# Two decode layers streamed through SBUF: one array for all records, more columns kept, a smaller ring and finer w2 pieces

## The chip, the cores and the metric

The kernel runs on one core of one Trainium2 chip. The time is device microseconds of one execution. Times of several executions are given as their median with the lowest and the highest.

## The reference

Four tokens (batch B = 4, one position each, D = 640) go through attention, an MLP, the same attention and the same MLP again; both rounds use the same weights and the same caches. All is float32.

```python
x = A_x
x = x + A(_layernorm(x));  x = x + B(_layernorm(x))
x = x + A(_layernorm(x));  x = x + B(_layernorm(x))

# A: 32 heads of 128; the last W = 1024 positions of each cache
q = x @ wq                                   # 640 x 4096
scores = einsum("bhqd,bhkd->bhqk", q, k) * 128 ** -0.5
o = einsum("bhqk,bhkd->bhqd", softmax(scores), v)
return o.reshape(B, 1, 4096) @ wo            # 4096 x 640
# B: w1 is 640 x 1728, w2 is 1728 x 640
return maximum(x @ w1, 0) @ w2
```

## The kernel before

**Records.** Everything that one head needs is one *record* of 128 partitions x 9472 columns of float32 (`REC`): 640 columns of query weights (from `WQ` = 0), 4096 of keys (from `K` = 640), 4096 of values (from `V` = 4736) and 640 of output weights (from `WO` = 8832). In HBM the array `rec` has one block per head, [32, 128, 9472], so that two partitions' rows of one record lie 9472 x 4 = 37,888 bytes apart. The MLP's weights are one array `wm` of 128 x 17280 columns: five chunks of w1 with 1728 columns each and then 54 tiles of w2 with 160 columns each (`FD`).

**Places.** SBUF holds five slots of one record each (`slot0` to `slot4`), a `ring` of 5344 columns, `kept` with the last 2176 columns of record 26 and `kept2` with the last 1664 columns of record 5. Round 0 goes through the records 0 to 31. Its last five (27 to 31) stay in the slots and are the first five of round 1, which then goes through 0 to 26; so they are loaded once, and what lies in `kept` and `kept2` isn't loaded a second time either.

**Loads.** All loads are issued by SP's queue in one fixed order, the list `items`. `pump()` (line 250) issues the list's first entry as soon as no live columns lie in its place, and stops at the first that has no room yet. `done()` (line 271) frees columns after the last instruction that reads them and calls `pump()`. Around the first MLP the places are few, because the slots hold the five records that stay: `MLP_RING` (line 69) cuts `wm` into 11 pieces that pass through the ring and through `spare`, 1536 columns of the values of record 31, which `park()` (line 290) copies into PSUM and `unpark()` (line 298) brings back later into the keys' columns of slot 2. `IN_RING` and `IN_SLOT` (lines 74 to 76) then place record 0 of round 1 in ring, spare and slots, and the loop over `places` (lines 225 to 238) fills the slots' parts with records 1 to 5 as they are freed. `ending()` (line 190) orders the last three records of a round in parts, so that their keys come ahead of their values.

**Compute.** Each engine runs its instructions in the order in which the program states them (`InOrder`, line 84). For each record `query` makes q by five matmuls with the record's query weights, `scores` makes eight matmuls with the keys, `softmax` is a maximum on VectorE and an exponential on ScalarE, `weights` transposes and scales the probabilities, `values` makes eight matmuls with the values, `picks` and `output_T` gather the head's output, and `project` adds its product with the output weights to `acc`. The main loop (line 469) runs these one record apart: scores of the next record, then values of this one, then the query of the one after. `busy` (line 315) issues matmuls whose result nobody reads; they read the keys of slot `home(LAST, 0)`, which is slot 2, or another one that is named.

`mlp` (line 417) goes through w1's chunks, then through w2 in groups of tiles: `W2_RING` (line 68) in round 0, `W2_SLOT` in round 1.

Of the kernel before, what the change touches and what calls it, by code (L numbers as in the profile page):

```python
# [32 lines left out]
F32 = mybir.dt.float32  # L33
# [5 lines left out]
P = 128  # L39
B, D, H, DH, W, FF = 4, 640, 32, 128, 1024, 1728  # L40
NB = 4
FD = D // NB
# [4 lines left out]
WQ, K, V, WO = 0, D, D + 4 * W, D + 8 * W  # L47
REC = 2 * D + 8 * W
HALF = REC // 2
VH = 2 * W  # L50

NS = 5
# [5 lines left out]
TCOLS = len(TILES) * FD  # L58
RING = 5344
KEPT = WO - 3 * 512  # L60
SIXTH = 5
KEPT2 = WO - 2 * 512
PARKED = 1536
# [14 lines left out]
CUTS = [*range(0, K, DH), *range(K, WO, 512), *range(WO, REC + 1, FD)]  # L78
W1_SLOT = [[0, 1], [2], [3], [4]]
# [26 lines left out]
def decode_kernel(ctx: ExitStack, tc: tile.TileContext, xf, rec, wm, out):  # L106
# [64 lines left out]
    def home(h, r):  # L171

        return h % NS if not r or h >= LAST else (h - 6 + LAST) % NS

# [3 lines left out]
    live = []  # L178
    spare = home(H - 1, 0)
    buffers = dict(enumerate(slot)) | {"ring": ring, "kept": kept, "kept2": kept2}  # L180

    def load(key, src, lo, hi, buf, col):
        if buf == "spare":
            buf, col = spare, V + col
        items.append((key, src, lo, hi, buf, col))

    def piece(r, h, lo, hi, buf=None, col=None):
        load(("rec", r, h), rec[h], lo, hi, home(h, r) if buf is None else buf, lo if col is None else col)

    def ending(r, hs, late):  # L190
        a, b, c = hs[-3:]
        end = WO if late else REC
        last = WO if late else KEPT
        for h, lo, hi in ((a, 0, V), (b, 0, V), (a, V, end), (c, 0, V), (b, V, end), (c, V, V + VH), (c, V + VH, last)):
            piece(r, h, lo, hi)
        if late:
            for h in hs[-1:] + hs[-LATE:-1]:
                if h == LAST - 1:
                    piece(r, h, WO, REC, "kept", WO - KEPT)
                else:  # L200
                    piece(r, h, WO, REC)
# [12 lines left out]
    for lo, hi, buf, col in MLP_RING:  # L214
        load(("w", 0), wm, lo, hi, buf, col)

# [5 lines left out]

    for lo, hi, buf, col in IN_RING:
        piece(1, new[0], lo, hi, buf, col)
    places = [(old[i], lo, hi) for i, lo, hi in (
        (0, 0, K), (0, K + 1024, K + VH), (0, K + VH + 512, V), (1, 0, K + VH), (1, K + VH, V), (0, V, WO), (0, WO, REC),
        (2, 0, V), (1, V, REC), (3, 0, V), (2, V, REC), (4, 0, V), (3, V, REC), (4, V + PARKED, REC),
        (4, V, V + PARKED))] + [("ring", 0, RING)]
    stream = [(new[0], lo, hi) for lo, hi in IN_SLOT] + [(h, 0, KEPT2 if h == SIXTH else REC) for h in new[1:6]]
    for buf, lo, hi in places:  # L230
        while stream:
            h, c, end = stream[0]
            cut = max(x for x in [*CUTS, end] if x <= min(end, c + hi - lo))
            if cut <= c:
                break
            piece(1, h, c, cut, buf, lo)
            lo += cut - c
            stream[:1] = [(h, cut, end)] if cut < end else []
    assert not stream
# [3 lines left out]
    for ks in W1_SLOT:  # L243
        load(("w", 1), wm, ks[0] * FF, (ks[-1] + 1) * FF, home(LAST + 1, 0), ks[0] * FF)
    n = 0
    for size in W2_SLOT:
        load(("w", 1), wm, W2 + n * FD, W2 + (n + size) * FD, home(LAST + 2, 0), n * FD)
        n += size

    def pump():  # L250

        while items:
            key, src, lo, hi, buf, col = items[0]
            if any(b == buf and x < col + hi - lo and col < y for b, x, y in live):
                return
            sp.dma_start(buffers[buf][:, col:col + hi - lo], src[:, lo:hi])
            live.append((buf, col, col + hi - lo))
            at.setdefault(key, []).append((lo, hi, buf, col))
            items.pop(0)
# [30 lines left out]
    def park(i):  # L290
        if i == 0:
            act.copy(sc_ps[1], slot[spare][:, V:V + 1024])
        else:
            act.copy(o_ps, slot[spare][:, V + 1024:V + PARKED])
            free(spare, V, V + PARKED)
            pump()

    def unpark(i):
        b = home(LAST, 0)
        a = [K, K + 512, K + VH][i]  # L300
        if i == 0:
            act.copy(slot[b][:, a:a + 512], sc_ps[1][:, :512])
        else:
            dve.tensor_copy(slot[b][:, a:a + 512], [sc_ps[1][:, 512:], o_ps][i - 1])
        live.append((b, a, a + 512))
        if i == 2:
            dve.memset(o_ps, 0.0)
            at["rec", 1, H - 1] = [(0, V, spare, 0), (V, V + 1024, b, K), (V + 1024, V + PARKED, b, K + VH),
                                   (V + PARKED, REC, spare, V + PARKED)]

# [3 lines left out]

    def busy(n, to=misc, groups=1, h=LAST):
# [29 lines left out]

    def query(r, h):
# [4 lines left out]
        dve.tensor_copy(qT, misc[:, 8:8 + B])  # L351

    def scores(r, h, s, first=False):
        key = ("rec", r, h)
        for i in range(2):
            for b in range(B):
                pe.matmul(sc_ps[s][32 * b:32 * b + 4, 512 * i:512 * i + 512], qT[:, b:b + 1].to_broadcast([P, 4]),
                          cols(key, K + 512 * (B * i + b), 512), start=True, stop=True)
# [58 lines left out]
    def mlp(r):  # L417
# [38 lines left out]
    for r in range(2):  # L456
# [4 lines left out]
        if r:  # L461
            busy(256, t_ps, 2)
        scores(r, hs[0], 0, True)
# [5 lines left out]
        for n, h in enumerate(hs[:-2]):  # L469
# [3 lines left out]
            softmax(s)  # L473
            end = n == H - 3
            values(r, h)
            if end:
                for _ in range(3):
                    busy(512)
            picks(0)
            query(r, hs[n + 2])  # L480
            if end:
                scores(r, hs[-1], 1)
                weights(s, (0,))
            if r and n < NS - 2:
                busy(256, sc_ps[n % 2], 2, H - 1)
            output_T(max(i, 0), by_act=end)
# [65 lines left out]
```

## Time and profile before

| | |
|---|---|
| median of 3 runs | 714.66 us (713.81 to 715.4) |
| profiled execution, its own time | 713.95 us |
| its span, first to last instruction | 712.2 us |
| busy: PE, PE weight loads, VectorE, ScalarE | 512.9, 208.7, 358.5, 95.9 us |
| DMA | 302.53 MB, mean 425 GB/s |
| mean granted TensorE clock | 0.805 |

Busy times are unions over the whole span and overlap one another. All instructions bear line 98 (or 95), where the helper `InOrder` issues them, so groups are told apart by the names of the tiles that they write and read (out<-in). `slot<-rec` is a load of a record's columns into a slot, `ring<-wm` one of MLP weights into the ring. `PEclk` is the granted clock as a share of full speed.

### The profile page before, as it was taken

The numbers are of one execution on the slowest core, as the hardware profiler recorded it, in microseconds if no ns is written. First come the engines' busy times: TensorE is split into PE (matmuls) and PEld (weight loads), VectorE is DVE, ScalarE is ACT, GpSimd is POOL, SyncE is SP. The second block draws the span as 40 slices with busy tenths as digits, with TensorE's granted clock in tenths as the row PEclk, the third lists the DMA queues.
The fourth block names the chain that finished last, engine by engine and source line by source line (L and its number), as shares of the span: only waits on it lengthen the run. The fifth ranks groups of instructions, "written<-read, shape, count | busy, mean of one in ns | idle before, by whom it ended". The sixth has DMA issues, their size and how long they took to land.

```text
span 712.2 us, 8977 instructions
## 1 busy us (share of the span) xinstructions
PE 512.9 (72%) x3718; PEld 208.7 (29%) x3718; DVE 358.5 (50%) x1008; ACT 95.9 (13%) x152; POOL 1.1 (0%) x9
## 2 busy tenths in 40 slices
PE   4466668676586756768989899776858666677976
PEld 2132223223233222323223333232323222233322
DVE  3335444544454545447541877744445544444761
ACT  1201010110101011011120321201010110101111
POOL 0000000000000000000000000000000000000000
PEclk9778786877876687678899999976686878866899
DMA  9999999999999999999999999999999999999996
GB/s 375 443 435 426 428 437 440 418 437 438 433 420 443 433 429 428 430 436 428 424 403 396 418 432 428 441 432 433 433 434 433 430 431 435 432 431 425 429 424 286
DMA packets 16633, 302.53 MB, mean 425 GB/s; under 512 B 1856, under 2 KB 2512, under 8 KB 6992
## 3 DMA queue, kind: packets, MB, share of 16 engines
q1 hardware_dynamic: 16560, 301.95, 99.1%
q8 instruction: 29, 0.48, 0.2%
q14 instruction: 12, 0.10, 0.0%
q10 hardware_dynamic: 32, 0.01, 0.0%
HBM read 301.87 MB, written 0.08 MB: 424 GB/s over the span
## 4 chain that ended last, share of the span: by engine, by line
DMA 81%; PE 15%; DVE 2%; issue 1%; ACT 0%; SPq 0%
DMA slot<-rec 75%; PE misc L98 5%; PE sc_ps L98 4%; PE o_ps L98 4%; DMA ring<-wm 3%; DMA slot<-wm 3%; PE acc L98 3%; DVE scratch L98 1%; DVE oTs L98 1%; DVE small L98 0%; ACT sc_ps L98 0%; PE t_ps L98 0%; SPq L98 0%; DVE t_ps L98 0%; ACT t_ps L98 0%
## 5 line engine op out<-in xcount | busy, mean ns | idle before, releaser
L98 PE MATMUL misc<-xT,slot 128*128 128x4 f32 x640 | 104.2, 290 | 153.9 <-DMA slot<-rec 153.5
L98 PE MATMUL sc_ps<-slot,qT 128*4 128x512 f32 x1014 | 194.5, 898 | 1.9 <-DVE qT L98 1.1
L98 PEld LDWEIGHTS misc<-xT,slot 128*128 128x128 f32 x640 | 98.6, 238 | 211.2 <-DMA slot<-rec 200.4
L98 ACT ACTIVATE sc_ps<-sc_ps,small 128x1024 f32<-128x1024 f32 (+1 forms) x68 | 76.6, 1127 | 536.1 <-DVE small L98 535.6
L98 PE MATMUL o_ps<-slot,scratch 128*16 128x512 f32 x956 | 129.0, 652 | 2.4 <-DVE scratch L98 2.1
L98 DVE TENSOR_REDUCE small<-sc_ps 128x1 f32<-128x1024 f32 x64 | 78.3, 1223 | 70.5 <-PE sc_ps L98 70.4
L98 DVE COPY qT<-misc 128x4 f32<-128x4 f32 x64 | 10.2, 160 | 171.5 <-PE misc L98 171.3
L98 DVE STREAM_TRANSPOSE t_ps<-sc_ps 128x512 f32<-128x512 f32 x128 | 93.2, 728 | 2.1
L98 DVE SCALAR_TENSOR_TENSOR scratch<-o_ps,of_block,scratch 128x128 f32<-128x128 f32 x186 | 65.2, 351 | 6.6
L98 PEld LDWEIGHTS o_ps<-slot,scratch 128*16 128x16 f32 x956 | 31.5, 115 | 118.0 <-issue 70.7
L98 PEld LDWEIGHTS sc_ps<-slot,qT 128*4 128x4 f32 x1014 | 33.7, 114 | 83.7 <-issue 73.2
L98 PE MATMUL acc<-slot,oTs 128*4 128x160 f32 x478 | 35.7, 384 | 13.8 <-DVE oTs L98 13.3
L98 DVE TENSOR_SCALAR scratch<-o_ps,of_block 128x128 f32<-128x128 f32 x62 | 21.7, 350 | 28.9 <-PE o_ps L98 28.9
L98 PE MATMUL o_ps<-pick,scratch 128*128 128x4 f32 x124 | 28.6, 301 | 4.9 <-DVE scratch L98 4.9
L98 DVE TENSOR_TENSOR scratch<-t_ps,mrt 128x64 f32<-128x64 f32 x128 | 28.8, 225 | 4.7
L98 PEld LDWEIGHTS o_ps<-pick,scratch 128*128 128x128 f32 x124 | 25.3, 253 | 11.6 <-DVE scratch L98 8.1
L98 PE MATMUL misc<-slot,small 128*1 128x512 f32 (+1 forms) x40 | 19.5, 594 | 1.6 <-DMA slot<-rec 1.6
L98 DVE COPY oTs<-o_ps 128x4 f32<-128x4 f32 x58 | 9.4, 162 | 13.7 <-PE o_ps L98 12.7
L98 DVE TENSOR_SCALAR mrt<-of_batch,small 128x4 f32<-128x4 f32 x64 | 14.7, 230 | 2.2
L98 DVE STREAM_TRANSPOSE scratch<-small 128x32 f32<-128x32 f32 x64 | 12.9, 202 | 1.1 <-ACT sc_ps L98 1.0
L98 PEld LDWEIGHTS acc<-slot,oTs 128*4 128x4 f32 x478 | 6.8, 84 | 19.2 <-DVE oTs L98 18.0
L98 ACT ACTIVATION_READ_ACCUMULATOR sc_ps<-sc_ps,small 128x1 f32 x64 | 12.2, 191 | 0.0
(76 smaller groups left out, 122.6 us busy)
## 6 DMA issues: line engine op xcount, KB each, us to landing
slot<-rec SPq DMA_DIRECT2D x42, 4736.0 KB, 30.7
slot<-rec SPq DMA_DIRECT2D x15, 2368.0 KB, 20.7
slot<-rec SPq DMA_DIRECT2D x2, 4416.0 KB
slot<-rec SPq DMA_DIRECT2D x2, 2048.0 KB, 40.7
slot<-rec SPq DMA_DIRECT2D x4, 1024.0 KB, 8.9
slot<-rec SPq DMA_DIRECT2D x1, 3904.0 KB
slot<-rec SPq DMA_DIRECT2D x1, 3648.0 KB, 34.0
ring<-wm SPq DMA_DIRECT2D x4, 864.0 KB, 6.7
```

Source lines behind the costliest of these rows:

```text
L98: r = build(*args, **kwargs)
```

## The change

It has six parts.

- **Layout.** The array of records is transposed on the host to [128, 32 x 9472], and the five slots become one tile `store` of 5 x 9472 columns. Two partitions' rows now lie 1,212,416 bytes apart. A load is a run of columns that may cross from one record into the next (`run`, `weight`).
- **Kept columns and ring.** `kept2` holds the last 2688 columns of record 5 instead of 1664; the ring has 4320 columns instead of 5344.
- **Refill.** The lists `MLP_RING`, `W2_RING`, `IN_RING` and `IN_SLOT` are cut anew: `wm` passes in 13 pieces instead of 11, w2's groups have 2, 5, 9, 8, 10, 9, 7 and 4 tiles instead of 8, 11, 9, 10, 11 and 5. In round 1 the records of index 5 and on go one slot further than before (`home`).
- **Last query.** In each round the 640 columns of query weights of the last record are loaded ahead of the values of the record two before; its query is made ahead of those `values`, into `qT2` in `scratch`, and its scores ahead of `picks`.
- **Fillers.** `busy` always reads `kept`. There are four instead of three at the end of a round, five instead of four between the groups of w2 in round 0, and those before the first scores of round 1 are 128 columns wide instead of 256.
- **Names.** `park`, `unpark` and `pump` address columns of `store` in place of a slot.

```diff
-RING = 5344
+RING = 10 * FQ
-KEPT2 = WO - 2 * 512
+KEPT2 = WO - 4 * 512
...
-W2_RING = [8, 11, 9, 10, 11, 5]
-MLP_RING = [(0, 1728, "ring", 0), (1728, 3456, "ring", 1728), (3456, 5184, "ring", 3456), (5184, 6480, "spare", 0),
-            (6480, 8208, "ring", 0), (8208, W2 + 1280, "ring", 1728), (W2 + 1280, W2 + 3040, "ring", 3456),
-            (W2 + 3040, W2 + 4480, "spare", 0), (W2 + 4480, W2 + 6080, "ring", 0), (W2 + 6080, W2 + 7840, "ring", 1600),
-            (W2 + 7840, WM, "ring", 3456)]
-
-IN_RING = [(640, 1664, "ring", 4256), (1664, 3200, "spare", 0), (3200, 4736, "ring", 0), (4736, 6272, "ring", 1536),
-           (6272, 7296, "ring", 3072), (8832, 8992, "ring", 4096)]
-IN_SLOT = [(0, K), (7296, WO), (8992, REC)]
+W2_RING = [2, 5, 9, 8, 10, 9, 7, 4]
+MLP_RING = [(0, 1728, "ring", 0), (1728, 3456, "ring", 1728), (3456, 4320, "ring", 3456), (4320, 5616, "spare", 0),
+            (5616, 7344, "ring", 0), (7344, W2 + 320, "ring", 1728), (W2 + 320, W2 + 1120, "ring", 3456),
+            (W2 + 1120, W2 + 2560, "spare", 0), (W2 + 2560, W2 + 3840, "ring", 0), (W2 + 3840, W2 + 5440, "ring", 1280),
+            (W2 + 5440, W2 + 6880, "ring", 2880), (W2 + 6880, W2 + 8000, "spare", 0), (W2 + 8000, WM, "ring", 0)]
+
+IN_RING = [(0, 2176, "ring", 640), (2176, 3200, "ring", 2816), (8832, 9312, "ring", 3840), (3200, 4736, "spare", 0),
+           (4736, 5248, "ring", 0)]
+IN_SLOT = [(5248, WO), (9312, 5 * REC + KEPT2)]
...
+    qT2 = scratch[:, 416:420]
...
-    slot = [sb.tile([P, REC], F32, name=f"slot{i}") for i in range(NS)]
+    store = sb.tile([P, NS * REC], F32, name="store")
...
-        return h % NS if not r or h >= LAST else (h - 6 + LAST) % NS
+        return h % NS if not r or h >= LAST else (h - 5 + LAST) % NS
...
+    def run(r, lo, hi, buf, col):
+
+        parts = [(("rec", r, h), max(lo - h * REC, 0), min(hi - h * REC, REC), col + max(h * REC - lo, 0))
+                 for h in range(lo // REC, (hi - 1) // REC + 1)]
+        load(rec, lo, hi, buf, col, parts)
...
-        for h, lo, hi in ((a, 0, V), (b, 0, V), (a, V, end), (c, 0, V), (b, V, end), (c, V, V + VH), (c, V + VH, last)):
+        for h, lo, hi in ((a, 0, V), (b, 0, V), (c, 0, K), (a, V, end), (c, K, V), (b, V, end), (c, V, V + VH),
+                          (c, V + VH, last)):
...
-            pe.matmul(to[32 * g:32 * g + 1, :n], ones, slot[home(h, 0)][:, K:K + n],
+            pe.matmul(to[32 * g:32 * g + 1, :n], ones, kept[:, :n],
...
-            if r == 0 and i < len(sizes) - 2:
+            if r == 0 and i < len(sizes) - 3:
...
-            busy(256, t_ps, 2)
+            busy(128, t_ps, 2)
...
             end = n == H - 3
+            if end:
+                query(r, hs[-1], qT2)
             values(r, h)
             if end:
-                for _ in range(3):
+                for _ in range(4):
                     busy(512)
+                scores(r, hs[-1], 1, q=qT2)
             picks(0)
-            query(r, hs[n + 2])
             if end:
-                scores(r, hs[-1], 1)
                 weights(s, (0,))
+            else:
+                query(r, hs[n + 2])
...
-        "rec": rec,
+        "rec": rec.transpose(1, 0, 2).reshape(P, H * REC),
```

More of the change, by code (lines that the diff above doesn't have):

```diff
@@ L178, in decode_kernel, with load, weight, piece @@
     live = []
[L179 to L188, printed above, removed]
+    spare = home(H - 1, 0) * REC + V
+    first = home(LAST, 0) * REC
+    buffers = {"store": store, "ring": ring, "kept": kept, "kept2": kept2}
+    def load(src, lo, hi, buf, col, parts):
+        items.append((src[:, lo:hi], buf, col, hi - lo, parts))
+    def weight(r, lo, hi, buf, col):
+        load(wm, lo, hi, buf, col, [(("w", r), lo, hi, col)])
+    def run(r, lo, hi, buf, col):
+        parts = [(("rec", r, h), max(lo - h * REC, 0), min(hi - h * REC, REC), col + max(h * REC - lo, 0))
+                 for h in range(lo // REC, (hi - 1) // REC + 1)]
+        load(rec, lo, hi, buf, col, parts)
+    def piece(r, h, lo, hi, buf="store", col=None):
+        run(r, h * REC + lo, h * REC + hi, buf, home(h, r) * REC + lo if col is None else col)
     def ending(r, hs, late):
@@ L214, in decode_kernel @@
     for lo, hi, buf, col in MLP_RING:
-        load(("w", 0), wm, lo, hi, buf, col)
+        weight(0, lo, hi, *(("store", spare + col) if buf == "spare" else (buf, col)))
     hs = order[1]
@@ L223, in decode_kernel @@
     for lo, hi, buf, col in IN_RING:
-        piece(1, new[0], lo, hi, buf, col)
-    places = [(old[i], lo, hi) for i, lo, hi in (
+        run(1, lo, hi, *(("store", spare + col) if buf == "spare" else (buf, col)))
+    places = [("store", old[i] * REC + lo, old[i] * REC + hi) for i, lo, hi in (
         (0, 0, K), (0, K + 1024, K + VH), (0, K + VH + 512, V), (1, 0, K + VH), (1, K + VH, V), (0, V, WO), (0, WO, REC),
         (2, 0, V), (1, V, REC), (3, 0, V), (2, V, REC), (4, 0, V), (3, V, REC), (4, V + PARKED, REC),
-        (4, V, V + PARKED))] + [("ring", 0, RING)]
-    stream = [(new[0], lo, hi) for lo, hi in IN_SLOT] + [(h, 0, KEPT2 if h == SIXTH else REC) for h in new[1:6]]
+        (0, K, K + 1024), (0, K + VH, K + VH + 512), (4, V, V + PARKED))] + [("ring", 0, RING)]
+    stream = list(IN_SLOT)
     for buf, lo, hi in places:
         while stream:
-            h, c, end = stream[0]
-            cut = max(x for x in [*CUTS, end] if x <= min(end, c + hi - lo))
+            c, end = stream[0]
+            cut = max(x for x in [h * REC + x for h in new[:6] for x in CUTS] + [end] if x <= min(end, c + hi - lo))
             if cut <= c:
                 break
-            piece(1, h, c, cut, buf, lo)
+            run(1, c, cut, buf, lo)
             lo += cut - c
-            stream[:1] = [(h, cut, end)] if cut < end else []
+            stream[:1] = [(cut, end)] if cut < end else []
     assert not stream
@@ L252, in pump @@
         while items:
-            key, src, lo, hi, buf, col = items[0]
-            if any(b == buf and x < col + hi - lo and col < y for b, x, y in live):
+            src, buf, col, n, parts = items[0]
+            if any(b == buf and x < col + n and col < y for b, x, y in live):
                 return
-            sp.dma_start(buffers[buf][:, col:col + hi - lo], src[:, lo:hi])
-            live.append((buf, col, col + hi - lo))
-            at.setdefault(key, []).append((lo, hi, buf, col))
+            sp.dma_start(buffers[buf][:, col:col + n], src)
+            live.append((buf, col, col + n))
+            for key, lo, hi, c in parts:
+                at.setdefault(key, []).append((lo, hi, buf, c))
             items.pop(0)
@@ L291, in park, with busy @@
         if i == 0:
-            act.copy(sc_ps[1], slot[spare][:, V:V + 1024])
+            act.copy(sc_ps[1], store[:, spare:spare + 1024])
         else:
-            act.copy(o_ps, slot[spare][:, V + 1024:V + PARKED])
-            free(spare, V, V + PARKED)
+            act.copy(o_ps, store[:, spare + 1024:spare + PARKED])
+            free("store", spare, spare + PARKED)
             pump()
     def unpark(i):
-        b = home(LAST, 0)
-        a = [K, K + 512, K + VH][i]
+        a = first + [K, K + 512, K + VH][i]
         if i == 0:
-            act.copy(slot[b][:, a:a + 512], sc_ps[1][:, :512])
+            act.copy(store[:, a:a + 512], sc_ps[1][:, :512])
         else:
-            dve.tensor_copy(slot[b][:, a:a + 512], [sc_ps[1][:, 512:], o_ps][i - 1])
-        live.append((b, a, a + 512))
+            dve.tensor_copy(store[:, a:a + 512], [sc_ps[1][:, 512:], o_ps][i - 1])
+        live.append(("store", a, a + 512))
         if i == 2:
             dve.memset(o_ps, 0.0)
-            at["rec", 1, H - 1] = [(0, V, spare, 0), (V, V + 1024, b, K), (V + 1024, V + PARKED, b, K + VH),
-                                   (V + PARKED, REC, spare, V + PARKED)]
+            at["rec", 1, H - 1] = [(0, V, "store", spare - V), (V, V + 1024, "store", first + K),
+                                   (V + 1024, V + PARKED, "store", first + K + VH),
+                                   (V + PARKED, REC, "store", spare + PARKED)]
     back = sc_ps[0][:, 512:768]
     pad = back[:, 208:240]
-    def busy(n, to=misc, groups=1, h=LAST):
+    def busy(n, to=misc, groups=1):
         for g in range(groups):
-            pe.matmul(to[32 * g:32 * g + 1, :n], ones, slot[home(h, 0)][:, K:K + n],
+            pe.matmul(to[32 * g:32 * g + 1, :n], ones, kept[:, :n],
                       start=True, stop=True)
@@ L344, in xblock, with query @@
         return xT[:, 32 * k:32 * k + B]
-    def query(r, h):
+    def query(r, h, to=qT):
         key = ("rec", r, h)
@@ L350, in query, with scores @@
         done(key, WQ, K)
-        dve.tensor_copy(qT, misc[:, 8:8 + B])
-    def scores(r, h, s, first=False):
+        dve.tensor_copy(to, misc[:, 8:8 + B])
+    def scores(r, h, s, first=False, q=qT):
         key = ("rec", r, h)
@@ L356, in scores @@
             for b in range(B):
-                pe.matmul(sc_ps[s][32 * b:32 * b + 4, 512 * i:512 * i + 512], qT[:, b:b + 1].to_broadcast([P, 4]),
+                pe.matmul(sc_ps[s][32 * b:32 * b + 4, 512 * i:512 * i + 512], q[:, b:b + 1].to_broadcast([P, 4]),
                           cols(key, K + 512 * (B * i + b), 512), start=True, stop=True)
```

8 lines of the change are left out of this document (4 added, 4 removed).

## The prediction

> **What bounds the kernel now.** I read the slices of the span first, then the queues, then the chain that ended last, and only then single stretches.
>
> ```profile
> DMA  9999999999999999999999999999999999999996
> q1 hardware_dynamic: 16560, 301.95, 99.1%
> DMA 81%; PE 15%; DVE 2%; issue 1%; ACT 0%; SPq 0%
> ```
>
> The DMA engines are busy in every slice but the last; the packets of one queue took 99.1% of sixteen engines' span (705.8 of 712.2 us) for 301.95 MB; the chain that ended last is 81% DMA. So the kernel is a stream of loads, and an edit moves the time only through the number of bytes, the rate at which they move, and stretches in which the DMA engines have nothing issued. Now the stretches (start:end, length, busy time and count of PE, PEld, DVE, ACT, POOL, then PEclk, DMA share, GB/s):
>
> ```profile
> 35.00:70.00 35.00, 22.20 (x156) 9.24 (x156) 16.66 (x46) 3.89 (x6) 0.00 (x0) 0.80 1.00 430
> 342.00:360.00 18.00, 16.02 (x86) 4.16 (x85) 10.37 (x29) 2.75 (x5) 0.00 (x0) 0.81 0.99 420
> 360.00:378.00 18.00, 15.42 (x123) 4.18 (x124) 5.60 (x21) 3.39 (x6) 0.00 (x0) 0.91 1.01 394
> 378.00:392.00 14.00, 12.68 (x165) 5.70 (x162) 2.50 (x11) 1.62 (x4) 0.00 (x0) 1.00 1.01 406
> 392.00:410.00 18.00, 15.95 (x150) 6.74 (x146) 15.83 (x43) 5.67 (x9) 0.00 (x0) 1.00 1.03 420
> 470.00:510.00 40.00, 29.01 (x186) 10.92 (x178) 19.27 (x52) 5.18 (x8) 0.00 (x0) 0.71 1.00 433
> 685.00:706.00 21.00, 16.56 (x164) 5.36 (x160) 10.03 (x31) 4.28 (x9) 0.00 (x0) 1.00 0.98 413
> ```
>
> Where whole records stream (470:510) the rate is 433 GB/s, and that is as fast as it gets here. It falls to 394 and 406 around the first MLP (360 to 392), with the DMA share still at 1.01: the engines have packets in hand, but shorter ones. The two ends of the chain, in order of time (start, length, what):
>
> ```profile
> 327.18 33.13 DMA slot<-rec
> ...
> 360.34 8.88 DMA ring<-wm
> ...
> 369.25 1.37 PE sc_ps L98 x8
> ...
> 370.64 6.35 DMA ring<-wm
> ...
> 379.67 6.17 DMA ring<-wm
> ...
> 684.83 21.27 DMA slot<-wm
> ...
> 706.14 2.34 PE acc L98 x60
> ...
> 708.50 0.50 PE acc L98 x8
> ```
>
> Around the first MLP the chain hops from one load into the ring to the next. At the end it runs on loads of `wm` to 706.10 and then through the last matmuls to 709.0; the span ends at 712.2. That tail hangs on the last landings and is not touched by the change, so what the stream gains, the span gains.
>
> **Part by part.** *Bytes.* `kept2` holds 1664 columns of record 5 now and 2688 afterwards, and what it holds is not loaded again in round 1.
>
> ```profile
> kept<-rec SPq DMA_DIRECT2D x1, 832.0 KB
> ```
>
> This is that load now: 1664 columns x 128 partitions x 4 bytes = 832 KB, so the columns price as in the code. The 1024 more columns save 1024 x 128 x 4 = 524,288 bytes of the second pass; at 433 GB/s that is 1.21 us. Nothing else alters the sum of bytes: all other records and both passes over `wm` are loaded in full as before.
>
> *More pieces.* Counting the load list in the code, 115 DMAs of SP become 118: the last record of each round is cut once more (640 columns of query weights first), the MLP's refill has 13 pieces where it had 11, and the start of round 1 has one piece fewer, because a piece may now cross from one record into the next. A price for one packet: at 433 GB/s the 301.95 MB would take 697.3 us, the queue took 705.8, so 8.5 us over 16560/16 = 1035 packets of an engine, at most 8.2 ns each. Three DMAs are 3 x (128 rows + 16 completions)/16 = 27 packets of an engine: +0.22 us. SP issues one after the other in 0.43 us (three in 1.28), and it has room:
>
> ```profile
> 386.91 1.28 SPq L98 DMA_DIRECT2D ring<-rec  x3
> SPq L98 <- PE acc L98: 452.4, 48, 21.6
> ```
>
> It sat 452.4 us waiting for PE to free space, so three more issues cost nothing unless the queue in front of the DMA engines runs dry, which is the next term.
>
> *A smaller ring.* The first MLP and the start of round 1 stream through the ring and 1536 parked columns: 6880 columns now, 5856 after. At 433 GB/s and 512 bytes a column and partition set this is 8.13 us of stream now and 6.92 us after: every refill has to be issued up to 1.21 us sooner after the columns' last use. Is there so much room? (KB of one, median us from issue to landing:)
>
> ```profile
> ring<-wm SPq DMA_DIRECT2D x4, 864.0 KB, 6.7
> ring<-wm SPq DMA_DIRECT2D x2, 880.0 KB, 5.6
> ring<-wm SPq DMA_DIRECT2D x1, 856.0 KB, 6.3
> slot<-wm SPq DMA_DIRECT2D x1, 720.0 KB, 5.8
> out<-scratch SPq DMA_DIRECT2D x1, 80.0 KB, 1.6
> ```
>
> The output's 80 KB need 0.19 us at 433 GB/s and land 1.6 us after their issue, so an issue into an empty queue costs about 1.4 us beside its bytes. The tightest refill, 880 KB, needs 2.08 + 1.4 = 3.5 us and took 5.6: it stood 2.1 us behind other transfers. The 864 KB ones: 6.7 - 2.04 - 1.4 = 3.3 us. Take 1.21 us off: 0.9 us stay in the tightest place. I take this term as zero. Its bounds: below, the whole shortfall of the two slow stretches, 18 x (1 - 394/433) + 14 x (1 - 406/433) = 2.5 us, less what short packets explain (12 pieces x 9 packets x 8.2 ns = 0.9 us), a gain of 1.6 us at best if the finer pieces smooth it; above, 1.21 us for each of the 17280/5856 = 2.95 fillings, 3.6 us, if there were no room at all. Zero lies nearest to the tightest row, which leaves 0.9 us of cover.
>
> *The last query ahead.* Matmuls near the end of round 0:
>
> ```profile
> 350.63 1.28 PE L98 MATMUL misc<-xT,slot 128*128 128x4 f32 x10 [0.69 <-DMA slot<-rec]
> 352.25 3.38 PE L98 MATMUL sc_ps<-slot,qT 128*4 128x512 f32 x16 [0.35 <-DVE scratch L98]
> 355.57 0.55 PE L98 MATMUL o_ps<-pick,scratch 128*128 128x4 f32 x2
> ...
> 360.21 1.05 PE L98 MATMUL sc_ps<-slot,scratch 128*16 128x512 f32 x8 [0.27 <-DVE scratch L98]
> ```
>
> The last query waits for a load until 350.63 and the scores begin at 352.25. With the 640 columns loaded first and the query ahead of `values`, the scores can begin as their keys land: 1.6 us sooner, and the softmax and the weights behind them too. But the chain does not pass there: it goes from `DMA slot<-rec` straight to `DMA ring<-wm`, and the MLP's first chunks wait for loads. What is late next is the last half of V and then the first chunk of w1, both bytes of the same stream. Worth on the path: zero. If that cover were absent, it would be the full 1.6 us in each of two rounds. Behind the moved query wait `values` of the record before, whose V is now loaded after these 640 columns; so it cannot be held up longer than by its own data.
>
> *Fillers.* They read `kept`, loaded long before, instead of a slot, which frees that slot for loads; one more in each round's end and one more in the W2 loop, 594 ns each:
>
> ```profile
> L98 PE MATMUL misc<-slot,small 128*1 128x512 f32 (+1 forms) x40 | 19.5, 594 | 1.6 <-DMA slot<-rec 1.6
> ```
>
> They stand where PE waits for a load; without that cover three of them would be 1.8 us. Zero on the path. In round 1 the filler before the first scores is halved, a few tenths of a microsecond of PE, also covered.
>
> *Layout.* All records become one array of 128 rows; a partition's rows of one load lie 32 x 37,888 = 1,212,416 bytes apart in HBM instead of 37,888. No row of this trace has such a pitch. Gain: excluded, since the whole-record rate of 433 GB/s is the same in 35:70 and 470:510 to 1%, a limit that does not depend on where in the run it is read. Loss: the lowest of the windows above that streams long pieces is 413 GB/s (685:706, `wm`, pitch 70,400 bytes), 4.8% under 433. I take zero, as both pitches that the trace does show reach over 410 GB/s with the DMA share near 1. The Trainium skill's page "DMA: Bandwidth & Descriptors", section "Latency and other measured facts", says that row pitches at large powers of two lose rate (214 GB/s full, 207 at 512 KiB, 164 at 2 MiB, 103 at 4 MiB). This pitch is 37 x 32 KiB, no power of two; by that rule read strictly the sum stays, by its 512 KiB figure taken as an estimate it would grow by some 3%, and no run here shows it.
>
> **The sum.** -1.21 + 0.22 = -0.99 us. The profiled execution took 713.95 us (span 712.2 and 1.75 around it) and would take 712.96. The median of the three runs is 714.66, 0.7 above the profiled one, so the median goes to 713.7.
>
> **Rivals.** *The refill starves (slower).* If PE frees columns over 0.9 us later relative to the stream than it does now, each refill reaches empty DMA engines. For it: the chain already hops from ring load to ring load. Against: 5.6 us from issue to landing for 3.5 us of need. Price up to 3.6 us: 714.66 - 0.99 + 3.6 = 717.3; from 1.0 us of loss on it eats the gain. Chance 0.19.
>
> *The pitch slows every load (slower).* Sixteen engines read rows that lie a fixed distance apart; if these fall on the same part of the HBM, every record pays. For it: nothing in this trace; against: two unlike pitches stream well. Price: 301.4 MB at 424 instead of 433 GB/s, halfway to the 413 row, is 14.8 us: 728.5. It decides early: 0.15% of the rate are 1.0 us and cancel the gain. This is the mechanism that the Trainium skill's page named above describes. Chance 0.13.
>
> *The first MLP streams better (faster).* With pieces of 2 to 10 tiles and the slots free of fillers, the 1.6 us of unexplained shortfall come back: 712.1. For it: 394 GB/s where 433 are possible. Against: a DMA share of 1.01 there. Chance 0.18. That the change does not do what it says is hardly possible: the columns held are not in the load list.
>
> **How the numbers follow.** Forecast 0.50, at 713.7, its own range 712.7 to 714.7 (the two bounds of packet price and the spread of medians, 713.81 to 715.4, about its middle). 0.2%, about what a measurement of this kernel can tell from no change, is 1.43 us, so the forecast itself mostly lies within: I give it 0.18 faster, 0.32 same. Smoother MLP: 0.18, of which 0.16 faster and 0.02 same. Starving: 0.05 same, 0.14 slower. Pitch: 0.13 slower. Together faster 0.34, same 0.39, slower 0.27. The range goes from 711.8 (the smoother MLP, less the 0.3 of spread) to 717.6 (starving in full and the same 0.3); the pitch and the outer edges lie outside.
>
> **What would show it.** Right: `kept<-rec` with one load of 1344 KB, 0.52 MB less on the queue, 433 GB/s where whole records stream, the last landing about 1 us earlier, the chain still on loads from the ring. Wrong: under 430 GB/s in 35:70 or 470:510 (pitch); issue-to-landing near 3.5 us for ring loads and a DMA share below 0.95 between 360 and 410 (starving); over 410 GB/s in 360 to 392 (smoother).

## The result: slower by a quarter of a per cent

The changed kernel took 716.6 us in the median (714.5 to 717.64), beside 714.05 us (713.76 to 717.08) for the kernel before in the same measurement: a ratio of 1.0025, with a 95% interval of 1.0015 to 1.0034. A later comparison gave 715.5 against 714.02, ratio 1.0013 (1.0002 to 1.0023). So the change costs about 1 to 2 us by the ratios (2.6 and 1.5 by the medians) where I had forecast a gain of 1.0. The time lies inside the range that I gave, the direction is the wrong one. Its profiled execution took 717.6 us (span 715.9), 3.65 us over the 713.95 of before.

The page of the changed kernel, its queue and the parts of the chain that ended last, then its table of loads (KB of one, median us from issue to landing):

```profile
q1 hardware_dynamic: 16992, 301.42, 98.7%
...
DMA 81%; PE 16%; DVE 2%; issue 1%; ACT 0%; SPq 0%
```

```profile
kept<-rec SPq DMA_DIRECT2D x1, 1344.0 KB
...
ring<-wm SPq DMA_DIRECT2D x3, 864.0 KB, 4.5
```

What was to be saved was saved: 0.53 MB fewer on the queue, and `kept2` loaded as 1344 KB. But the packets now took 98.7% of a longer span, 706.6 us in place of 705.8, and a refill of 864 KB landed 4.5 us after its issue where it had taken 6.7: it stands behind other transfers for a far shorter time. The stretches of the changed kernel (start:end, length, busy time and count of PE, PEld, DVE, ACT, POOL, then PEclk, DMA share, GB/s):

```profile
35.00:70.00 35.00, 23.19 (x168) 10.27 (x168) 16.38 (x47) 3.89 (x6) 0.00 (x0) 0.80 1.00 430
342.00:360.00 18.00, 15.56 (x94) 4.16 (x86) 12.11 (x34) 3.77 (x6) 0.00 (x0) 0.91 1.00 423
360.00:378.00 18.00, 16.78 (x115) 4.98 (x116) 3.84 (x16) 2.33 (x4) 0.00 (x0) 0.72 0.91 347
378.00:392.00 14.00, 11.00 (x135) 3.88 (x133) 1.61 (x5) 1.08 (x3) 0.00 (x0) 1.00 0.92 345
392.00:410.00 18.00, 16.23 (x143) 7.38 (x140) 13.92 (x40) 6.05 (x9) 0.00 (x0) 1.00 1.01 403
470.00:510.00 40.00, 30.05 (x197) 12.45 (x200) 19.34 (x55) 3.89 (x6) 0.00 (x0) 0.72 1.01 435
```

Whole records stream as before (430 and 435 GB/s beside 430 and 433), and so does the end of round 0 (423 beside 420). The loss lies in three neighbouring rows: 347 in place of 394, 345 in place of 406, 403 in place of 420, with a DMA share of 0.91 and 0.92 in place of 1.01. In bytes, 18 x 47 + 14 x 61 + 18 x 17 = 2006 KB (thousands of bytes) less moved between 360 and 410 us; at 433 GB/s that is 4.63 us. Take off the 1.21 us of bytes that need not be loaded, and 3.4 of the 3.65 us of the profiled executions are found.

Now what PE sees there. The timeline of PE (start, length, operation, in brackets the idle time before and what ended it), first of the kernel before, then of the changed one:

```profile
378.89 0.73 PE L98 MATMUL acc<-ring,scratch 128*4 128x160 f32 x16 [0.40 <-DVE scratch L98]
...
385.88 1.51 PE L98 MATMUL acc<-ring,scratch 128*4 128x160 f32 x31 [0.68 <-DMA ring<-wm]
...
388.60 1.28 PE L98 MATMUL misc<-xT,slot 128*128 128x4 f32 x10
...
464.94 2.12 PE L98 MATMUL misc<-xT,slot 128*128 128x4 f32 x10 [5.05 <-DMA slot<-rec]
```

```profile
378.96 0.47 PE L98 MATMUL acc<-ring,scratch 128*4 128x160 f32 x8 [0.41 <-DVE scratch L98]
...
381.61 0.84 PE L98 MATMUL acc<-store,scratch 128*4 128x160 f32 x17 [0.23 <-DMA store<-wm]
...
383.37 0.73 PE L98 MATMUL acc<-ring,scratch 128*4 128x160 f32 x16 [0.18 <-DMA ring<-wm]
...
386.63 1.00 PE L98 MATMUL acc<-ring,scratch 128*4 128x160 f32 x24 [1.70 <-DMA ring<-wm]
...
389.74 0.72 PE L98 MATMUL acc<-store,scratch 128*4 128x160 f32 x14 [0.38 <-DMA store<-wm]
...
392.07 1.28 PE L98 MATMUL misc<-xT,store 128*128 128x4 f32 x10
...
469.03 1.23 PE L98 MATMUL misc<-xT,store 128*128 128x4 f32 x5 [5.60 <-DMA store<-rec]
```

Both kernels begin w2 at the same time (378.89 and 378.96), yet the first query of round 1 comes at 392.07 in place of 388.60: group after group of w2 waits for its tiles. And 70 us later PE waits over 5 us for a record in either kernel. So it isn't PE's own lateness that is paid at the end; the stream of loads has lost time and doesn't get it back.

The chain of the changed kernel (start, length, what) says the same:

```profile
375.93 7.39 DMA ring<-wm
383.37 0.50 PE acc L98 x8
383.88 6.58 DMA ring<-wm
...
688.75 21.28 DMA store<-wm
710.07 2.84 PE acc L98 x68
```

A load into the ring, the matmuls that free a place, the next load: the ring is a loop of load and use. The last landing was to come 1 us earlier and came at 710.03, 3.9 us later than before.

### The profile page after: what moved, and what is told of

Its sections match the earlier page's. It is cut to its first block, busy times and chain, and to the rows that moved or that the text cites. A ratio compares the mean times of both kernels' runs of the same rounds, so it can differ in the third digit from the quotient of the medians.

```text
span 715.9 us, 8988 instructions
## 1 busy us (share of the span) xinstructions
PE 515.6 (72%) x3724; PEld 207.6 (29%) x3724; DVE 358.8 (50%) x1008; ACT 95.9 (13%) x152; POOL 1.1 (0%) x9
## 2 busy tenths in 40 slices
DMA packets 17065, 302.01 MB, mean 422 GB/s; under 512 B 1904, under 2 KB 2176, under 8 KB 7296
## 3 DMA queue, kind: packets, MB, share of 16 engines
q1 hardware_dynamic: 16992, 301.42, 98.7%
## 4 chain that ended last, share of the span: by engine, by line
DMA 81%; PE 16%; DVE 2%; issue 1%; ACT 0%; SPq 0%
DMA store<-rec 76%; PE misc L98 5%; PE sc_ps L98 4%; PE o_ps L98 4%; DMA store<-wm 3%; PE acc L98 3%; DMA ring<-wm 2%; DVE scratch L98 1%; DVE oTs L98 1%; PE t_ps L98 0%; DVE small L98 0%; ACT sc_ps L98 0%; DVE store L98 0%; SPq L98 0%; DVE t_ps L98 0%
## 5 line engine op out<-in xcount | busy, mean ns | idle before, releaser
L98 PE MATMUL misc<-xT,store 128*128 128x4 f32 x630 | 101.2, 287 | 154.3 <-DMA store<-rec 154.1
L98 PE MATMUL sc_ps<-store,qT 128*4 128x512 f32 x976 | 190.9, 913 | 1.4 <-DVE qT L98 1.1
L98 PEld LDWEIGHTS misc<-xT,store 128*128 128x128 f32 x630 | 95.7, 235 | 211.3 <-DMA store<-rec 198.8
L98 PE MATMUL o_ps<-store,scratch 128*16 128x512 f32 x960 | 127.0, 644 | 3.1 <-DMA store<-rec 1.6
L98 PEld LDWEIGHTS o_ps<-store,scratch 128*16 128x16 f32 x960 | 31.2, 113 | 116.2 <-issue 71.4
L98 PEld LDWEIGHTS sc_ps<-store,qT 128*4 128x4 f32 x976 | 32.8, 114 | 82.1 <-issue 71.6
L98 PE MATMUL acc<-store,oTs 128*4 128x160 f32 x474 | 37.0, 397 | 14.2 <-DVE oTs L98 13.2
L98 PE MATMUL misc<-kept,small 128*1 128x512 f32 (+1 forms) x46 | 22.0, 589 | 0.0
L98 PEld LDWEIGHTS acc<-store,oTs 128*4 128x4 f32 x474 | 6.9, 85 | 20.4 <-DVE oTs L98 18.0
```

The lines of the kernel that those rows point to most:

```text
L98: r = build(*args, **kwargs)
```

## The experiments

Two theories stood after the result. *Cover*: with 1024 columns less, refills can't be issued early enough and the DMA engines run out of work. *Something else in the change*: the layout, the order of the last query, the cut of record 0, PE's fillers, or PE's clock.

**The ring undone.** The changed kernel with ring, `kept2`, lists and groups of before; layout, last query and fillers stay.

```diff
-RING = 10 * FQ
+RING = 5344
-KEPT2 = WO - 4 * 512
+KEPT2 = WO - 2 * 512
-W2_RING = [2, 5, 9, 8, 10, 9, 7, 4]
+W2_RING = [8, 11, 9, 10, 11, 5]
...
```

> The changed kernel with the ring of 5344 columns, 1664 kept columns and the old refill lists; layout, last query and fillers stay changed. If the smaller refill buffer is what lets the DMA engines run dry around the first MLP (theory: cover), the starved stretch from 360 to 392 us goes back to about 400 GB/s and the time to 714 us, within 0.1% of before. If the moved query and its idle PE are the cause by themselves, or the pitch of the rows, it stays near 716 us (+0.2% or more).

Measured: 713.97 us, ratio 1.0006 (0.9991 to 1.0021). Without the smaller ring and its lists most of the loss is gone, and what remains can't be told from zero. The interval overlaps that of the change (1.0015 to 1.0034), as one of the twelve executions took 719.65 us; but eight of the twelve were faster than the fastest of the change's 22 (714.5).

**The other parts, one by one.** The layout alone in the kernel before:

```diff
-        "rec": rec,
+        "rec": rec.transpose(1, 0, 2).reshape(P, H * REC),
```

> The kernel before with the records as one array of 128 rows in HBM (rows of one load 1,212,416 bytes apart) and nothing else changed. If the pitch costs rate, 433 GB/s in the whole-record stretches fall and the time rises by 2 us or more. If, as the changed kernel's 433 to 435 GB/s suggest, it costs nothing, the time is 714 us, within 0.1% of before.

714.3 us, 1.0002 (0.9991 to 1.0012). The last query's new order alone in the kernel before (loads, query and scores moved, and the fourth filler):

```diff
+            if end:
+                query(r, hs[-1], qT2)
             values(r, h)
...
-                for _ in range(3):
+                for _ in range(4):
                     busy(512)
+                scores(r, hs[-1], 1, q=qT2)
```

> The kernel before with only the last query's change: its 640 columns loaded first, its query ahead of the values, its scores ahead of picks, four fillers instead of three. If the moved query leaves PE idle ahead of the MLP and that costs time by itself (theory: clock by the moved query), the time rises by 1 us or more (+0.15%) and the clock is at half when the MLP begins in its profile. If the larger ring covers it (theory: cover), it stays within 0.1% of before.

713.87 us, 0.9996 (0.9987 to 1.0006). And the reverse, the changed kernel with the old order and three fillers:

```diff
-            if end:
-                query(r, hs[-1], qT2)
...
+            query(r, hs[n + 2])
             if end:
+                scores(r, hs[-1], 1)
```

> The changed kernel with the last query's order, its load order and the three fillers as before; ring, kept columns, refill lists and layout stay changed. If the moved query leaves PE the idle stretches in which the clock falls (theory: clock by the moved query), the time returns to about 713 us (-0.1%). If the smaller buffer alone is enough, it stays at 716 us or above (+0.2%), since PE is then 1 us later at the MLP.

715.6 us, 1.0018 (1.0006 to 1.0029), as the change itself. The first load of record 0, 2176 columns, cut in two:

```diff
-IN_RING = [(0, 2176, "ring", 640), (2176, 3200, "ring", 2816), ...
+IN_RING = [(0, 640, "ring", 640), (640, 2176, "ring", 1280), (2176, 3200, "ring", 2816), ...
```

> The changed kernel with its first load of round 1, 2176 columns, cut in two: 640 columns, whose place is free after the fourth group of w2, and 1536 behind the fifth. If that late single load starves the engines between 384 and 390 us (theory: cover; in the changed kernel's profile the DMA share there falls to 0.71), about 0.6 to 1.2 us come back: +0.1% against before instead of +0.25%. If the loss is made only by PE's clock in the w1 part (theory: clock), nothing changes: +0.25%.

715.62 us, 1.0013 (1.0 to 1.0026): between no effect and half a gain, not settled. So neither layout nor order nor this cut carries the loss.

**PE's fillers and its clock.** In the profiled execution of the change TensorE's granted clock was 0.72 in 360 to 378, where before it was 0.91, and the first refill, which waits for PE's first chunk of w1, was issued 1.45 us later. SP's timeline, before and after:

```profile
368.24 5.59 SPq L98 DMA_DIRECT2D ring<-wm  x3
```

```profile
369.69 4.58 SPq L98 DMA_DIRECT2D ring<-wm  x3
```

Was it the clock? Three later executions of the change had a clock of 1.0 from 360 to 378 us; they issued that refill at 368.38, 368.46 and 368.72, so about 1 us of the 1.45 went with the half clock of the first. Two more fillers at the end of round 0 were to hold it up:

```diff
+        if not r:
+            busy(512)
...
-        values(r, hs[-1], 1)
+        values(r, hs[-1], 1, (0, 0) if r else (1, 0))
```

> The changed kernel with two more fillers of 512 columns at the end of round 0, in PE's waits ahead of the last two records' values. If PE's clock, granted at half from 362.6 to 372.8 us in the changed kernel's profile, is what makes the refill late (theory: clock), the clock stays at 1.0 through the first MLP chunks, the DMA engines move about 400 GB/s there, and the time is 713 us (-0.1 to -0.2% against before), with little spread between executions. If the smaller buffer starves the engines whatever the clock, it stays at 716 us. If the fillers only delay PE, it gets slower than 717 us.

The clock stayed at full speed from 334 to 426 us in the profiled execution, and the DMA engines were still short of work. The row is 368 to 378 us, first of the kernel before, then of this one:

```profile
368.00:378.00 10.00, 8.96 (x47) 1.85 (x44) 0.48 (x3) 0.33 (x2) 0.00 (x0) 0.83 0.99 373
```

```profile
368.00:378.00 10.00, 8.13 (x56) 1.82 (x53) 0.90 (x4) 1.37 (x4) 0.00 (x0) 1.00 0.96 352
```

716.33 us, 1.0025 (1.0011 to 1.0038): no gain in the median, though the profiled execution itself took 714.54, the fastest of its twelve. Next, without the fillers between w2's groups, as shown here, and then also without those between w1's chunks:

```diff
-            if r == 0 and i < len(sizes) - 3:
-                busy(512)
```

> The changed kernel without the five fillers between the groups of w2 in round 0. Each holds PE for 0.86 us at full clock ahead of the next group. Theory cover: columns come free up to 0.8 us sooner per group and the engines run dry less, 0.5 to 1.5 us back: +0.05 to +0.2% against before. Theory clock: the fillers are what keeps the clock up in the w2 part; without them it falls there and the time rises by 1 us or more, +0.4%.

> The changed kernel without any filler inside the first MLP (three between w1's chunks, five between w2's groups). Theory cover: PE is free sooner after every chunk, and the time falls to 713.5 to 715 us (-0.1 to +0.15%). Theory clock: the clock falls to half inside the MLP, a chunk of w1 then takes 1.6 us instead of 0.9, the engines starve as before and the time stays at 716.5 us or rises.

716.0 us, 1.0021 (1.0012 to 1.0031), and 716.62 us, 1.0034 (1.0017 to 1.005). Taking these fillers out gains nothing that shows. The second kernel keeps two more fillers between w1 and w2, so it isn't free of them as its expectation says. Two single executions of the change as it is asked whether the time of an execution goes with the clock:

> The changed kernel as it is, another profiled execution. Theory clock: the executions differ in where PE's clock falls; one with a clock of 1.0 from 360 to 378 us takes about 714.5 to 715.5 us, one with 0.7 to 0.8 about 717 us or more. If the clock has no part in it, time and clock in that stretch do not go together.

> The changed kernel as it is, a third profiled execution, for the same comparison: clock at 1.0 from 360 to 378 us with 714.5 to 715.5 us, or 0.7 to 0.8 with 717 us or more.

They took 714.98 and 716.77 us, and the clock was 1.0 from 360 to 392 us in both. So 1.8 us of spread arose with the clock at 1.0 there. The half clock probably added to the loss in the first profile, but the loss is there without it. The Trainium skill, page "TensorE: Matmul & The Clock Gate", section "What's actually happening", says that the clock is decided in free-running windows of 3413 ns; the slow spell of the first profile, 362.59 to 372.83 us, is 10.24 us or three of them, which agrees.

**Is there cover in the kernel before?** Three more fillers at the start of the first MLP, in both kernels, make PE late:

```diff
+        for _ in range(0 if r else 3):
+            busy(512)
```

> The kernel before with three more fillers (matmuls of 512 columns whose result nobody reads) at the start of the first MLP: some 1.3 to 2.4 us of work more on TensorE (three matmuls at 0.44 to 0.8 us by the clock) ahead of the first refill. Cover theory: the larger ring absorbs most of it, as its slowest DMA engine lost next to nothing at the refills: ratio 0.9995 to 1.0012 (714.0 to 715.2). Rival, that the path goes through TensorE at the first MLP anyway: all of it is paid, 1.002 to 1.0034.

> The changed kernel with the same three fillers at the same place. Cover theory: there is no cover left, so nearly all of the 1.3 to 2.4 us is paid on top of 1.0025: ratio 1.004 to 1.006 (717 to 718.5), with the GB/s of 360 to 392 below those of the change. Rival, that the loss comes from elsewhere (short packets, the cut as such): no more than the kernel before pays for the same fillers, 1.0025 to 1.0035.

The kernel before took 716.44 us (715.19 to 718.86), 1.0034 (1.0021 to 1.0047); the changed one 718.96 us (717.16 to 721.42), 1.0066 (1.005 to 1.0081). My expectation that the larger ring absorbs it fell, and the changed kernel lost more than the 1.004 to 1.006 that I had put down for it. I had also put the three fillers too low, at 1.3 to 2.4 us: at full clock a filler of 512 columns holds PE for 0.86 us (two records, 0.43 us each), so three hold it for 2.6. The first refill was issued 2.08 us later (SP's timeline of the delayed kernel before, against 368.24), and its profiled execution took 716.26, 2.3 us more:

```profile
370.32 3.04 SPq L98 DMA_DIRECT2D ring<-wm  x3
```

In the changed kernel, which ran these fillers at the half clock, the refill came at 373.94, 4.25 us after the 369.69 of its first profile, and the execution took 721.42, 3.8 us more. So already the kernel before has no cover to speak of. The cover theory was wrong in one point: the change doesn't remove cover, there was none to remove. In both kernels a later PE is paid nearly in full; that a smaller ring is paid by the same path is my reading, and the bytes of the stretch bear it out further down.

**Half the step.** A ring of 4832 columns and 2176 kept columns of record 5, with lists of my own; then the same with smaller pieces:

```diff
-RING = 10 * FQ
+RING = 4832
-KEPT2 = WO - 4 * 512
+KEPT2 = WO - 3 * 512
-W2_RING = [2, 5, 9, 8, 10, 9, 7, 4]
+W2_RING = [4, 8, 9, 10, 10, 8, 5]
...
```

> The changed kernel with a ring half way between the two, 4832 columns, 2176 columns of record 5 kept, and refill lists cut for that ring (12 pieces of wm, w2 in groups of 4, 8, 9, 10, 10, 8 and 5 tiles). 0.26 MB are saved, 0.6 us at 433 GB/s. Theory cover: the refill has 7.5 us of columns instead of 6.9, half the loss is gone, and the time lies between the two kernels or below both: -0.05 to +0.15% against before. If the loss came from the moved query, the fillers or the one store tile, which all stay as changed, it remains at +0.25%.

```diff
-W2_RING = [4, 8, 9, 10, 10, 8, 5]
+W2_RING = [4, 8, 9, 5, 5, 5, 5, 4, 4, 5]
...
```

> The ring of 4832 columns of after_mid with its refill in smaller pieces (w2 in pieces of 640 to 800 columns in place of 1280 to 1600, the 2048 columns of keys in two) and w2's groups cut to match, so that columns are freed and issued earlier. Cover by the cut: back from 1.0039 to 1.000 to 1.0015. Size alone, or a loss that does not hang on when places come free: stays at 1.003 to 1.0045.

717.21 us, 1.0039 (1.0021 to 1.0057), and 717.9 us, 1.0044 (1.0027 to 1.0061). Both miss what the cover theory expected: it doesn't show that half the columns cost half, and finer pieces bring nothing back; the second lies in the range that I had given for "size alone". In the profiled execution of the first, round 1's first query came at 388.74, as early as before, and yet it took 715.71. So, as far as one profile tells, part of its loss lies behind the MLP's loads, where my lists also place records 0 and 1 anew; size and placing aren't separated by these two.

**What are the bytes worth?** The changed kernel loads the 1024 columns once more in the middle of round 1, into the ring, where nobody reads them:

```diff
     for h in new[6:-3]:
+        if h == SIXTH + 5:
+            run(1, SIXTH * REC + KEPT2, SIXTH * REC + KEPT2 + 1024, "ring", 0)
         piece(1, h, 0, REC)
```

> The changed kernel with one load more: the 1024 columns of record 5 that kept2 holds are loaded once more in the middle of round 1, into the ring, where nobody reads them; the ring stays at 4320 columns. If the bytes are worth what the prediction took, it is 1.2 us above the change (ratio to the kernel before 1.004 to 1.0045, about 717.2 to 717.5), and the smaller ring alone costs some 3 us. Rival, that round 1 has idle room for 0.52 MB and the bytes were worth nothing: the same as the change, 1.0025 (715.8 to 716.6).

> The changed kernel as it is, on the same chip as after_reload: 1.0025 within 0.001 of the kernel before, single executions between 714.5 and 717.7.

716.98 us, 1.0040 (1.0026 to 1.0054), beside 715.5 us, 1.0013 (1.0002 to 1.0023), for the change on the same chip: the bytes are worth 1.5 us by the medians, 1.9 by the ratios, with some 1.2 of uncertainty. The 1.21 of the prediction lies within that, and zero, the rival, lies outside. My other expectation missed narrowly: the change came out at 1.0013, not within 0.001 of 1.0025, and against that first 1.0025 the bytes would be worth only 1.1 us, which zero would also fit. The kernel that loads them again has the smaller ring without its gain; it is 2.9 us slower than before (1.9 to 3.9). As layout and order were worth nothing that shows, that is the price of the ring and its lists.

**One sum for all.** The row 360 to 410 us of several kernels, each in its own fence: before, the change, the ring undone, the delayed kernel before, the delayed change.

```profile
360.00:410.00 50.00, 44.04 (x428) 16.63 (x432) 23.93 (x74) 10.68 (x18) 0.00 (x0) 0.97 1.02 407
```

```profile
360.00:410.00 50.00, 44.01 (x388) 16.24 (x388) 19.38 (x60) 9.46 (x16) 0.00 (x0) 0.90 0.95 366
```

```profile
360.00:410.00 50.00, 42.16 (x406) 16.16 (x410) 20.94 (x67) 9.76 (x18) 0.00 (x0) 0.93 1.01 400
```

```profile
360.00:410.00 50.00, 43.21 (x398) 16.37 (x398) 20.74 (x66) 10.25 (x18) 0.00 (x0) 0.97 0.99 388
```

```profile
360.00:410.00 50.00, 45.01 (x372) 15.60 (x376) 17.12 (x55) 8.37 (x15) 0.00 (x0) 0.86 0.88 337
```

If the time is decided by what the stream loses here, then 713.95 + 50 x (407 - GB/s)/433, less 1.21 us where 1024 columns more are kept (0.61 for 512), should be the time of each profiled execution:

| kernel | GB/s, 360 to 410 us | worked out, us | profiled execution, us |
|---|---|---|---|
| before, last query ahead | 408 | 713.8 | 713.86 |
| ring undone | 400 | 714.8 | 714.59 |
| before, layout alone | 395 | 715.3 | 716.56 |
| half the step | 393 | 715.0 | 715.71 |
| change, more fillers at the end of round 0 | 391 | 714.6 | 714.54 |
| change, beside the reloading kernel | 390 | 714.7 | 715.74 |
| change, first single execution | 388 | 714.9 | 714.98 |
| before, PE delayed | 388 | 716.1 | 716.26 |
| change, last query in the old order | 382 | 715.6 | 716.75 |
| change, second single execution | 380 | 715.9 | 716.77 |
| change, columns loaded again | 380 | 717.1 | 716.98 |
| change, no fillers between w1's chunks nor w2's groups | 379 | 716.0 | 715.63 |
| change, no fillers between w2's groups | 377 | 716.2 | 716.12 |
| change, load of record 0 cut in two | 367 | 717.4 | 717.84 |
| change, first profile | 366 | 717.5 | 717.6 |
| half the step, finer | 366 | 718.1 | 719.33 |
| change, PE delayed | 337 | 720.8 | 721.42 |

Over 7.6 us the sum errs by at most 1.3 us; five executions took 0.9 to 1.3 us longer than it says. On either side nothing of the kind is seen: from 342 to 360 us the eighteen executions moved 419 to 423 GB/s, from 410 to 442 us 427 to 434. So the place of most of the loss is shown, for the executions of the change as for the experiments. That the ring's size, and not the cut of its lists, makes the loss there is not shown.

## Why the prediction was wrong

*What bounds the kernel* was read rightly (the stream), and so was most of the sum. *Bytes*, -1.21 us: held (1.5 by the medians of the reloading kernel and the change). *Layout*, 0: held, 1.0002 alone and 435 GB/s in whole records; the 3% that I had estimated from a figure of the Trainium skill's page "DMA: Bandwidth & Descriptors", section "Latency and other measured facts", for large pitches did not come, at a pitch that is no power of two. *The last query ahead*, 0: held within about 0.1%. *Fillers*, 0: nothing else shows, as the kernel with the ring undone keeps them and stays at 1.0006; they weren't run alone. *More pieces*, +0.22 us, is too small to be told alone. Two slips enter no sum: `wm` has a pitch of 17280 x 4 = 69,120 bytes, not 70,400, and 413 lies 4.6% under 433, not 4.8%.

The step that failed is *A smaller ring*, taken as zero. It measured 2.9 us together with its lists (1.9 to 3.9), inside the bounds that I gave (-1.6 to 3.6, the upper one for "no room at all"). I had worked out 2.1 us of room, by taking an unloaded landing of 3.5 us from the 5.6 us of the tightest refill. The delayed kernel before refutes that: an issue 2.08 us later cost 2.3 us. Time in the queue behind other transfers was no room, for two reasons that fit what the traces show. Landing counts the slowest of sixteen DMA engines, and these are far from level: of the first chunk of w1, issued at 357.95 us in the kernel before, the first engine was done at 363.47 and the last at 367.14. The load just ahead of the first refill was done at 369.21 on its first engine and at 372.89 on its last, and the refill was issued at 368.24: 0.97 us of work for the engine that was ahead, less than the 1.4 us that I had myself put down for an issue into an empty queue. (That 1.4 came from the output's store.) By its first engine that refill was done 3.8 us after its issue, and the tightest one, 880 KB issued at 373.50, 3.9 us after: the same 3.8 to 3.9 us as the first refill of the change's first profile and of both delayed kernels, where the DMA share shows the gap. Beside some 2 us of bytes that is an estimated 1.7 to 1.9 us from the issue for an engine that has nothing else to do. What looked like 2 us of waiting for the load as a whole was none for that engine. And the ring is a loop: in the kernel before the chain goes from a landing to PE and to the next issue already, so a delay is handed on from refill to refill and not taken up.

There is a simpler way to have seen it. A column moved from the ring to `kept2` saves its bytes once, but it also shortens by the same bytes what can be loaded ahead when PE sets the pace: 1024 columns, 1.21 us, each time. With no room, one filling is enough to cancel the gain, and there are nearly three. This is an argument, and no run counts the fillings: the 2.9 us lie between one (1.21) and all (3.6). I wrote down the 1.21 us and the 2.95 fillings, and set them aside for one row of a table.

The rival *the refill starves* came true, nearly by its time: 717.3 worked out for a kernel before at 714.66, 716.6 measured beside 714.05. That the time lies inside my range is owed to this rival and not to the forecast. Its signs came in part: in the first profile the landing was 4.5 us (3.5 forecast) and the DMA share 0.91 and 0.92 from 360 to 392 us, while in the three executions with the clock at 1.0 the first refill still took 5.5 to 5.7 us and the share of 360 to 410 us was 0.98 to 1.00. The rate was the better sign: 380 to 390 GB/s there in these three, where the kernel before has 407. Its condition, that PE frees columns over 0.9 us later, was not even needed: these three issued the first refill 0.14 to 0.48 us later than the kernel before. Its chance of 0.19 rested on room that wasn't there.

Open stays why executions of the change differ by 1.8 us with the clock at 1.0 in that stretch, whether the size or the cut of the lists makes the 2.9 us, whether size or placing makes the half step as dear as the whole one, and how much of the 2.9 us a better list could bring back; no version here is shown to beat the kernel before (its own with the last query ahead, 0.9996, can't be told from it).

## What to carry to other kernels

The queue time of a load was not slack here: before a buffer is made smaller, make the consumer late by the same time (a few idle matmuls) and see whether that is paid; if it is, the buffer has no room to give. Columns taken from the read-ahead to keep other bytes pay only if the saving exceeds what the shorter read-ahead costs; here 1.2 us stood against 2.9. And where a stream bounds a kernel, count the bytes that each stretch moved: here the deficit of one stretch of 50 us gave the time of every profiled execution to 1.3 us.

## What had not been expected of the hardware

Sixteen DMA engines that serve the same loads ran up to 3.7 us apart, so a mean DMA share of 1.01 doesn't say that each has work. A partition pitch of 1,212,416 bytes streamed at 435 GB/s, no slower than 37,888 bytes. And the same program spread from 714.5 to 717.64 us where the kernel before, by the same stream, had half of its executions between 713.76 and 714.05, though single ones of it reached 717.08 too.
